# Routing steps placed by traced durations, expert weights split again at each visit, and tiles 2 to 7 turned through DRAM

## The chip, the cores and the metric

The kernel runs on one core of a Trainium2 chip. The metric is the device time of one execution in microseconds; lower is better. The engines are named as in the profile: PE (TensorE matmuls), PEld (its weight loads), DVE (VectorE), ACT (ScalarE), POOL (GpSimd) and SP (SyncE, which here only issues DMAs).

## The reference

A short causal filter, then a mixture of experts in which every token goes to exactly one of eight experts, by a greedy walk through all logits with a capacity for each expert.

```python
B, S, d_model = 8, 3584, 192                  # 28672 tokens; 8 heads of 24 columns, 7 taps
w = softmax(weight)                            # (8, 7)
x = einsum('hk,bskhg->bshg', w, windows(x))    # each head mixes 7 tokens

logits = x @ w_gate                            # (28672, 8)
order = np.argsort(-logits.flatten())
for idx in order:                              # greedy, capacity 3584 for each expert
    tok, e = idx // 8, idx % 8
    if assigned[tok] >= 0 or counts[e] >= cap: continue
    assigned[tok] = e; counts[e] += 1
for e in range(8):
    out[assigned == e] = np.maximum(x[assigned == e] @ w1[e], 0) @ w2[e]   # 192 -> 1024 -> 192
```

## The kernel before

**Two stages.** First the filter: 16 half-batches of 1792 tokens, each with 8 heads (PE matmul cv, ACT copy a, a DMA of the result to attn in DRAM), and the gate's logits beside it (pl, then LT). Then the feed-forward part: 56 tiles of 512 tokens, numbered from 0. Tiles 0 to 7 take one tile from each expert 0 to 7, tiles 8 to 31 three from each expert 7 down to 0, tiles 32 to 55 three from each expert 0 to 7. In run, each tile has eight steps: in step f, PE computes one eighth of the first layer of tile i (l1: five matmuls into ph, then ACT's relu hh and VectorE's remainder hl) and half of a quarter of the second layer of tile i-1 (l2: eight matmuls into y). All numbers are split into a high and a low part, so that float32r matmuls are accurate enough.

**Routing.** Which token goes where is found by generators (half(0), tail, half(1), rest) whose steps are put between the other work: thresholds, counts, a sort by one-hot matmuls (sort for the first half, sort4 for the others), a table read back from DRAM (otab, tile OT), a gather matmul (asm) and the decoding into token numbers (tokens, which writes ia, ja, ib, jb). The matmuls of these steps write the tile bg. sort4 makes one-hot tiles oa on VectorE, multiplies them on PE, ACT copies the result to X, and S.dma_start writes it to otab.

**What sets their place.** Instructions stand on each engine in the order in which the program emits them. Pace keeps an estimate of the time on PE, DVE and ACT, from the cost of each instruction in Meter. Steps.hook emits routing steps as long as VectorE's estimate is not more than slack ahead of PE's. A generator can yield PEW: its next step then comes only when PE's estimate has passed that of VectorE plus lat (0.8 in the feed-forward part). bg.drain emits all that is left at once: idx_of calls it in step 0 of tile 6 for half(1) and in step 0 of tile 30 for rest, since the gathers of tiles 8 and 32 need the lists.

**Tokens.** gather fetches a tile's tokens to xg two tiles ahead, with four indirect DMAs on POOL. They have to be turned for l1. Three ways: PE transposes into px (transp, evac: tiles 0 to 7), a turn through DRAM (turn, where swapped(i) is true: tiles 8 to 31; one VectorE transpose in step 6 of tile i-2, four writes to scr and two reads back on SP, then ACT copies in step 3 and subtracts in step 4 of tile i-1, the one for xa on POOL), and VectorE transposes alone (shuffle: tiles 32 to 55). The turn through DRAM needs the rows of the token list in another order, which tokens makes with sixteen small VectorE instructions (swap).

**Weights.** plan lists the pieces of each expert's weights, eight for a visit. wload brings a piece as it is to one of four raw tiles (SP), wsplit makes the high part on ACT and the low part on the engine eng (VectorE from tile 0 on). At an expert's first visit the split pieces are also written to DRAM (kw, kd, kv), and a later visit loads them split. Two sets of buffers alternate between visits.

Of the kernel before, what the change touches and what calls it, by code (L numbers as in the profile page):

```python
# [28 lines left out]
class Meter:  # L29
# [5 lines left out]
    def __getattr__(self, op):  # L35
# [4 lines left out]
        def call(*a, **k):  # L40
# [4 lines left out]
            if self.name == "pe":  # L45
                n = size(aps[2])

                d = n / 2400 * (0.25 if bf and size(aps[1]) == 32 else 1 if aps[2].dtype in (BF, FR) or size(aps[1]) == 32 else 2 if op == "transpose" else 4)
                p.pe += max(d + 0.0025, 0.027 if bf else 0.107)
# [195 lines left out]
TA = 16  # L245
# [13 lines left out]
class Route:  # L259
# [167 lines left out]
    def columns(self, h, nt, base):  # L427
# [9 lines left out]
        V.tensor_copy(bi[:, 1], ps[:, 0:8])  # L437
        V.tensor_scalar(bi, bi, 8, None, op0=OP.arith_shift_right)
# [34 lines left out]
    def sort(self, h, nt, base, per=8):  # L473
# [7 lines left out]
        while z < 128:  # L481

            t = max(q[0][1] + nc.las, free[0] if z % 32 == 0 else 0.0) if q else 0.0
            if q and t <= nc.pe:
                if z == 64:
                    self.columns(h, nt, base)
# [25 lines left out]
    def sort4(self, h, nt, base):  # L512
# [9 lines left out]
        free = [0.0, 0.0]  # L522
        while z < 8:

            t = max(q[1][1] + nc.las, free[0]) if len(q) > 1 else 0.0
            if len(q) > 1 and t <= nc.pe:
                if z == 4:
                    self.columns(h, nt, base)
                ps = self.bg()
                for v in range(2):  # L530
                    a = q.pop(0)[0]
                    for u in range(2):
                        for c in range(4):
                            j = 2 * v + u
                            PE.matmul(ps[32 * c:32 * c + 32, 128 * j:128 * j + 128],
                                      b[:, :, 32 * (c % 2) + 4 * z + j], a[:, u, :, c],
                                      start=True, stop=True, skip_group_check=True)
                A.activation(O[z // 4][:, 4 * (z % 4):4 * (z % 4) + 4].rearrange("p g q -> p (g q)"), ps, AF.Copy)
                free = [free[1], nc.act + nc.las]
                z += 1  # L540
                if z % 4 == 0:
                    S.dma_start(self.otab[z // 4 - 1], O[z // 4 - 1])
# [54 lines left out]
    def tokens(self, nt, idx, row, e1=8, t1=None, swap=False):  # L597
# [30 lines left out]
        if swap:  # L628
            r4, y4 = (t.rearrange("p e (t b) -> p e t b", b=4) for t in (row, y))
            for q in range(4):  # L630
                for b in range(4):
                    V.tensor_scalar(r4[32 * q:32 * q + 32, :, :, b], y4[32 * b:32 * b + 32, :, :, q], 4.0, None,
                                    op0=OP.mult)
                yield
        else:
            V.tensor_scalar(row, y, 4.0, None, op0=OP.mult)
            yield
# [15 lines left out]
    def counts(self, n0):  # L653
# [23 lines left out]
        yield  # L677
# [181 lines left out]
    def final(self):  # L859
# [32 lines left out]
        yield  # L892
# [254 lines left out]
class FFN:  # L1147
# [3 lines left out]
    def __init__(self, tc, nc, attn, w1, w2, out, ident, wr, drm):  # L1151
        self.tc, self.nc = tc, nc

        self.kept1 = [drm.tile([128, 3, F], F32, name="kw%d" % e) for e in range(NE)]
        self.keptd = [drm.tile([64, F], F32, name="kd%d" % e) for e in range(NE)]
        self.scr = [drm.tile([6, 32, 4, 128], F32, name="scr%d" % j) for j in range(2)]
        self.kept2 = [drm.tile([128, 8, 2 * D], F32, name="kv%d" % e) for e in range(NE)]
# [19 lines left out]
    def plan(self, tiles):  # L1177
# [7 lines left out]
        self.pieces = []  # L1185
        for j, ky in enumerate(keys):
            w = last[keys[j - 2]] + 1 if j > 1 else j - 1
            if ky[0] in [k[0] for k in keys[:j]]:
                self.pieces += [(w, ky, j % 2, "W1", 0), (w + 1, ky, j % 2, "W2", 0)]
                continue  # L1190
            for what, q in (("a", 0), ("d", 0), ("a", 1), ("d", 1)):
                self.pieces.append((w, ky, j % 2, what, q))
            for q in range(4):
                self.pieces.append((w + 1, ky, j % 2, "w", q))
        self.loaded = self.done = 0

    def wload(self):
        nc = self.nc
        if self.loaded == len(self.pieces) or self.pieces[self.loaded][3] in ("W1", "W2"):
            return  # L1200
        _, (e, _), _, what, q = self.pieces[self.loaded]
# [13 lines left out]
    def wsplit(self, i, eng):  # L1215

        if self.done == len(self.pieces) or self.pieces[self.done][0] > i:
            return
        V, A = self.nc.vector, self.nc.scalar
        _, ky, j, what, q = self.pieces[self.done]  # L1220
        wp = self.wpa[j]
        e = ky[0]
        if what == "W1" or (what, q) == ("a", 0):
            W = wp.tile([128, 3, F], FR, name="w1")
            self.WT[ky] = [W[:, 0], W[:, 1], W[:, 2], self.DL[j]]
        if what == "W1":
            self.nc.sync.dma_start(W.bitcast(F32), self.kept1[e])
            self.nc.sync.dma_start(self.DL[j][0:64].bitcast(F32), self.keptd[e])
            self.done += 1
            return  # L1230
        if what == "W2":
            t = self.wpb[j].tile([128, 8, 2 * D], FR, name="w2")
            self.WT[ky].append(t)
            self.nc.sync.dma_start(t.bitcast(F32), self.kept2[e])
            self.done += 1
            return
# [465 lines left out]
```

## Time and profile before

| | us |
|---|---|
| median of 3 runs | 1257.85 (1257.07 to 1260.27) |
| the profiled execution, its own time | 1263.32 |
| its span, first to last instruction | 1261.5 |
| PE busy | 1211.2 |
| DVE busy | 974.1 |
| ACT busy | 548.5 |
| POOL busy | 534.1 |

Busy time of PE is modelled from pipelined matmuls. L55 is the line of the helper that records each instruction, so almost all of VectorE's, ScalarE's and TensorE's work has that line, and the names of the tiles tell the operations apart (in the changed kernel the helper's line is L56). In a waits row the numbers are: us in total, how many times, the longest.

### The profile page before, as it was taken

Reading aid. Unit: us, or ns where it says so; the run is one execution under the profiler, and the core shown is the slowest. Engines: PE = TensorE matmul, PEld = TensorE weight load, DVE = VectorE, ACT = ScalarE, POOL = GpSimd, SP = SyncE. Lnnn points to the kernel's source line nnn. Section 1 sums busy time; section 2 is a strip of 40 time slices with the busy share of each in tenths; the row PEclk is TensorE's granted clock in tenths of the full one; section 3 lists DMA queues with packets and bytes.
Section 4 is the critical chain, followed back from the end, with each engine's and each line's share of the span. In section 5 each row is a group of like instructions: output and inputs, shape, how many; then the busy total and the mean of one; then the engine's idle time right before and its main releaser. Section 6 shows DMA issues by size and latency. Waiting matters only on the chain.

```text
span 1261.5 us, 21753 instructions
## 1 busy us (share of the span) xinstructions
PE 1211.2 (96%) x7702; PEld 1038.5 (82%) x7702; DVE 974.1 (77%) x2131; ACT 548.5 (43%) x1220; POOL 534.1 (42%) x528
## 2 busy tenths in 40 slices
PE   5989998999899999999899999999999999999997
PEld 2445567889799889888788999999999999999997
DVE  7398579899799999989885444777777777777772
ACT  4544655565345435454343333333333333333332
POOL 3000434354455454544534555444444444444422
PEclk9999999999899999999999999999999999999999
DMA  9999898899734443635274645113143232414100
GB/s 240 351 322 311 264 333 281 268 325 283 269 98 132 131 144 118 195 89 185 80 201 131 189 117 171 42 48 130 61 153 105 93 100 98 145 52 150 48 23 28
DMA packets 125188, 205.09 MB, mean 163 GB/s; under 512 B 21440, under 2 KB 85392, under 8 KB 121360
## 3 DMA queue, kind: packets, MB, share of 16 engines
q1 hardware_dynamic: 82464, 127.22, 31.6%
q0 software_dynamic: 21504, 44.07, 11.6%
q10 hardware_dynamic: 21104, 32.34, 7.8%
q8 instruction: 62, 1.02, 0.3%
q14 instruction: 54, 0.44, 0.1%
HBM read 118.64 MB, written 84.93 MB: 161 GB/s over the span
## 4 chain that ended last, share of the span: by engine, by line
PE 75%; DVE 13%; DMA 5%; issue 3%; SPq 1%; POOL 1%; ACT 1%; another core or an unknown queue 0%; DVEq 0%; POOLq 0%; ACTq 0%
PE ph L55 35%; PE y L55 34%; DVE X L55 4%; PE cv L55 3%; DVE hl L55 2%; PE bg L55 2%; DMA raw<-in_moe_w_dram 2%; DMA X<-in_x_dram 1%; DMA wgr<-in_moe_w_gate_dram 1%; DVE aT L55 1%; PE pl L55 1%; DVE oa L55 1%; DVE yo L55 1%; DMA kw<-w 0%; POOL xg L1269 0%
## 5 line engine op out<-in xcount | busy, mean ns | idle before, releaser
L55 PE MATMUL y<-w,hh 128*128 128x384 f32 x1792 | 537.7, 355 | 0.0
L55 ACT ACTIVATE hh<-ph 128x512 fp32r<-128x512 f32 x448 | 268.0, 598 | 478.3 <-PE ph L55 432.3
L55 PE MATMUL y<-w,hl 128*128 128x192 f32 x1792 | 449.6, 251 | 0.0
L55 DVE SCALAR_TENSOR_TENSOR hl<-ph,hh 128x512 fp32r<-128x512 f32 x448 | 307.6, 687 | 156.6 <-ACT hh L55 131.5
L55 PE MATMUL ph<-xa,w 128*128 128x512 f32 x1344 | 396.8, 403 | 0.7 <-DVE hl L55 0.6
L55 PEld LDWEIGHTS y<-w,hl 128*128 128x128 f32 x1792 | 341.9, 191 | 16.6
L55 PEld LDWEIGHTS y<-w,hh 128*128 128x128 f32 x1792 | 337.4, 188 | 22.0 <-issue 3.4
L1344 POOL DMA_INDIRECT out_dram<-yo,ia x128 | 142.5, 1113 | 258.7 <-DVE yo L55 222.4
L55 PEld LDWEIGHTS ph<-xa,w 128*128 128x128 f32 x1344 | 219.1, 189 | 21.8 <-issue 1.5
L1344 POOL DMA_INDIRECT out_dram<-yo,ib x96 | 96.0, 1000 | 220.0 <-DVE yo L55 212.6
L55 PE MATMUL ph<-xd,w 128*128 128x512 f32 x448 | 178.2, 398 | 1.1 <-DVE xd L55 1.1
L55 PE MATMUL ph<-xd,dl 128*128 128x512 f32 x448 | 174.9, 390 | 0.2 <-issue 0.2
L55 DVE STREAM_TRANSPOSE xs<-xg 32x128 f32<-32x128 f32 (+2 forms) x408 | 164.8, 404 | 6.6
L1269 POOL DMA_INDIRECT xg<-attn,ja x128 | 138.8, 1085 | 47.7 <-issue 39.0
L55 ACT ACTIVATE yt<-y 128x192 f32<-128x192 f32 x224 | 73.2, 327 | 103.5 <-PE y L55 84.8
L55 PE MATMUL cv<-X,TH 118*128 118x384 f32 x256 | 100.9, 520 | 16.9 <-DMA X<-in_x_dram 13.7
L1269 POOL DMA_INDIRECT xg<-attn,jb x96 | 103.5, 1078 | 29.3 <-issue 29.3
L55 DVE TENSOR_TENSOR yo<-y,yt 128x192 f32<-128x192 f32 x224 | 79.0, 353 | 41.7 <-ACT yt L55 37.6
L55 PEld LDWEIGHTS ph<-xd,w 128*128 128x128 f32 x448 | 84.4, 188 | 25.2 <-issue 4.7
L55 PEld LDWEIGHTS ph<-xd,dl 128*128 128x128 f32 x448 | 84.6, 189 | 20.2 <-issue 0.5
L55 PEld LDWEIGHTS cv<-X,TH 118*128 118x128 f32 x256 | 45.1, 197 | 50.4 <-issue 14.6
L55 ACT ACTIVATE a<-cv 128x384 f32<-128x384 f32 x128 | 59.8, 492 | 54.5 <-PE cv L55 41.8
(238 smaller groups left out, 886.1 us busy)
## 6 DMA issues: line engine op xcount, KB each, us to landing
attn<-a ACTq DMA_DIRECT2D x16, 1344.0 KB
w<-kw SPq DMA_DIRECT2D x14, 1536.0 KB
w<-kv SPq DMA_DIRECT2D x14, 1536.0 KB
kw<-w SPq DMA_DIRECT2D x48, 256.0 KB
kv<-w SPq DMA_DIRECT2D x32, 384.0 KB
X<-in_x_dram SPq DMA_DIRECT2D x17, 672.0 KB
X<-in_x_dram ACTq DMA_DIRECT2D x15, 672.0 KB
scr<-xs SPq DMA_DIRECT2D x96, 96.0 KB
```

Source lines behind the costliest of these rows:

```text
L55: return f(*a, **k)
L1269: self.nc.gpsimd.indirect_dma_start(out=t[:, b], out_offset=None, in_=self.attn[0:rows], in_offset=bass.IndirectOffsetOnAxis(ap=idx[b], ax ...
L1344: st = self.nc.gpsimd.indirect_dma_start(out=self.out, out_offset=bass.IndirectOffsetOnAxis(ap=idx, axis=0), in_=o, in_offset=None, bounds ...
```

## The change

It has four parts.

- Costs of the planner. VectorE: 0.15 + n/960 instead of the larger of 0.08 + n/960 and 0.18; ScalarE: 0.22 + n/1370 instead of 0.12 + n/1400; float32r matmuls 17/16 of before. Four waits PEW are added: in columns, after its first two instructions, in counts, in final, and so in sort and sort4, which call columns.
- sort4 emits its matmuls in four groups of 64, each when four one-hot tiles are there, instead of eight groups of 32 with two.
- Tiles 2 to 7 are turned through DRAM too. The first list (ja0) therefore gets the other row order, after a small list j2 for tiles 0 and 1 in the old order.
- kw, kd and kv are gone. Every visit loads raw pieces and splits them, later visits with the subtract on POOL, and with the next raw load issued two wsplit calls later (owed). A visit whose buffer still holds that expert (experts 6 and 1) loads nothing (same).

```diff
-                p.dve = max(p.dve, p.pe) + max(0.08 + n / 960 / w, 0.18)
+                p.dve = max(p.dve, p.pe) + 0.15 + n / 960 / w
             else:
-                p.act = max(p.act, p.pe) + 0.12 + n / 1400 + (0.2 if "accum_out" in k else 0)
+                p.act = max(p.act, p.pe) + 0.22 + n / 1370 + (0.2 if "accum_out" in k else 0)
...
         V.tensor_copy(bi[:, 1], ps[:, 0:8])
+        yield PEW
...
-            t = max(q[1][1] + nc.las, free[0]) if len(q) > 1 else 0.0
+            t = max(q[3][1] + nc.las, free) if len(q) > 3 else 0.0
...
+            if j > 1 and keys[j - 2][0] == ky[0]:
+                self.same[ky] = self.same.get(keys[j - 2], keys[j - 2])
+                continue
             w = last[keys[j - 2]] + 1 if j > 1 else j - 1
-            if ky[0] in [k[0] for k in keys[:j]]:
-                self.pieces += [(w, ky, j % 2, "W1", 0), (w + 1, ky, j % 2, "W2", 0)]
-                continue
+            again = ky[0] in [k[0] for k in keys[:j]]
...
+        self.turns += 1
+        while self.owed and self.owed[0] <= self.turns:
+            self.owed.pop(0)
+            self.wload()
...
+        if again:
+            eng = self.nc.gpsimd
...
         eng.tensor_tensor(lo, r[0:n], hi[0:n].bitcast(F32), op=OP.subtract)
-        S = self.nc.sync
-        if what == "w":
-            S.dma_start(self.kept2[e][:, s], t[4][:, s].bitcast(F32))
...
+        self.done += 1
+        if again:
+            self.owed.append(self.turns + 2)
         else:
-            S.dma_start(self.kept1[e][:, 2, s], hi.bitcast(F32))
-            S.dma_start(self.keptd[e][:, s], lo.bitcast(F32))
-        self.done += 1
-        self.wload()
+            self.wload()
...
     def swapped(self, i):
-        return self.tiles[i][1][1] in (1, 2, 3)
+        return i > 1 and self.tiles[i][1][1] < 4
...
         def first():
             for e in range(2):
-                ff.gather(e, [ja0[:, e, b:b + 1] for b in range(4)], NTOK // 2, P)
+                ff.gather(e, [j2[:, e, b:b + 1] for b in range(4)], NTOK // 2, P)
+            drain(r.swapped(ja0, r.y))
```

Where the steps stand then. In the filter, four of the five count matmuls of the threshold move one to three heads later. half(1) has its sort in tiles 3 and 4 instead of tile 2, its gather in tile 4 instead of tile 3. The first round has its matmuls in tile 9 instead of 7, the last two sorts stand in tiles 27 to 29 instead of 22 to 24.

On PE, at the end of routing, before: the end of the step that precedes the last gather (bg from iq and then from c_oh), in tile 24. The last sort matmuls stand five steps earlier.

```order
L55 MATMUL ph<-xa,w_7098 128x512 x3
L55 MATMUL ph<-xd,w_7098 128x512
L55 MATMUL ph<-xd,dl 128x512
L55 MATMUL y<-w_7355,hh 128x384
L55 MATMUL y<-w_7355,hl 128x192
...
L55 LDWEIGHTS ones
L55 MATMUL bg<-iq,ones 128x192
L55 LDWEIGHTS X_8487
L55 MATMUL bg<-c_oh,X_8487 128x24
```

And in the changed kernel, at the end of tile 29: the first row is the last matmul of the last sort; between it and the gather stand eight y matmuls, of which two are shown.

```order
L56 MATMUL bg<-oa,X_9192 32x128
L56 MATMUL y<-w_7892,hh 128x384
L56 MATMUL y<-w_7892,hl 128x192
...
L56 LDWEIGHTS ones
L56 MATMUL bg<-iq,ones 128x192
L56 LDWEIGHTS X_9655
L56 MATMUL bg<-c_oh,X_9655 128x24
```

The distance from the last sort to the gather has shrunk from five steps to half a step.

On SP, in one of the first tiles, before: raw loads, each behind the writes of the piece split before.

```order
L1255 DMA kw_87<-w_2991 128x512
L1256 DMA kw_87<-w_2991 128x512
L1210 DMA raw<-in_moe_w_dram 128x2x192
L1258 DMA kw_87<-w_2991 128x512
L1259 DMA kd_95<-dl 64x512
L1210 DMA raw<-in_moe_w_dram 128x2x192
```

And in the changed kernel, around step 6 of one of the first tiles:

```order
L1222 DMA raw<-in_moe_w_dram 128x2x192 x2
L1392 DMA scr_83<-xs 32x6x128 x4
L1394 DMA xs<-scr_83 128x512
L1395 DMA xs<-scr_83 64x512
L1222 DMA raw<-in_moe_w_dram 128x2x192 x2
L1217 DMA raw<-in_moe_w_dram 128x512
```

The writes to kw, kd and kv are gone, and one raw load a tile now stands behind the six transfers of the turn.

On POOL, before, around tile 11: the gather of four indirect DMAs (xg), the scatters of results (out_dram) and the subtract for xa.

```order
L1269 DMA xg<-attn,ja 128x192 x4
L1344 DMA out_dram<-yo,ia 28672x192 x2
L1403 TENSOR_TENSOR xa<-xs,xa 128x512
L1344 DMA out_dram<-yo,ia 28672x192 x2
L1269 DMA xg<-attn,ja 128x192 x4
```

And in the changed kernel, tile 11:

```order
L1269 DMA xg<-attn,ja 128x192 x4
L1256 TENSOR_TENSOR w_4696<-raw,w_4696 128x512
L1344 DMA out_dram<-yo,ia 28672x192
L1256 TENSOR_TENSOR dl<-raw,w_4696 64x512
L1256 TENSOR_TENSOR w_4696<-raw,w_4696 128x512
L1344 DMA out_dram<-yo,ia 28672x192
L1256 TENSOR_TENSOR dl<-raw,w_4696 64x512
L1403 TENSOR_TENSOR xa<-xs,xa 128x512
L1344 DMA out_dram<-yo,ia 28672x192 x2
```

Four subtracts for the weights have come in between the gather and the subtract for xa.

More of the change, by code (lines that the diff above doesn't have):

```diff
@@ L485, in sort @@
                 if z == 64:
-                    self.columns(h, nt, base)
+                    yield from self.columns(h, nt, base)
                 a = q.pop(0)[0]
@@ L1318, in l2 @@
         hh, hl = self.H[i]
[L1319 removed]
+        w = self.wt(key)[4]
         if half == 0:
```

106 lines of the change are left out of this document (49 added, 57 removed).

## The prediction

> **What bounds the kernel now.** I read the page first, for the share of each engine and the chain that ended last.
>
> ```profile
> span 1261.5 us, 21753 instructions
> PE 1211.2 (96%) x7702; PEld 1038.5 (82%) x7702; DVE 974.1 (77%) x2131; ACT 548.5 (43%) x1220; POOL 534.1 (42%) x528
> PE 75%; DVE 13%; DMA 5%; issue 3%; SPq 1%; POOL 1%; ACT 1%; another core or an unknown queue 0%; DVEq 0%; POOLq 0%; ACTq 0%
> ```
>
> TensorE is busy for 96% of the span and is three quarters of the chain, so time changes only where PE works longer, waits, or runs at a lower clock. To see where, I cut the feed-forward part into windows whose edges are the starts of a tile's first ph matmul in the timeline. A tile has 104 matmuls of its own (40 into ph, 64 into y). The columns are the window, its length, then busy time and count for PE, PEld, DVE, ACT, POOL, and the granted clock, the DMA share and GB/s.
>
> ```profile
> 175.88:199.96 24.08, 22.16 (x146) 19.07 (x146) 19.17 (x46) 11.76 (x25) 3.65 (x5) 1.00 0.89 314
> 199.96:227.58 27.62, 25.45 (x244) 21.17 (x243) 26.66 (x52) 15.37 (x30) 15.12 (x9) 1.00 0.85 275
> 269.17:288.36 19.19, 19.19 (x114) 17.36 (x113) 18.95 (x40) 14.24 (x38) 11.04 (x10) 1.00 0.95 325
> 288.36:307.57 19.21, 19.21 (x114) 17.37 (x113) 18.73 (x47) 10.60 (x22) 7.20 (x8) 1.00 0.96 310
> 307.57:332.71 25.14, 21.95 (x112) 19.52 (x111) 20.39 (x49) 10.29 (x23) 12.50 (x12) 0.86 0.84 272
> 332.71:600.98 268.27, 265.65 (x1538) 238.35 (x1536) 249.19 (x573) 126.61 (x322) 138.86 (x126) 1.00 0.45 140
> 600.98:629.65 28.67, 25.37 (x218) 21.60 (x216) 24.28 (x57) 9.81 (x20) 14.04 (x14) 0.94 0.28 79
> 629.65:654.17 24.52, 24.30 (x239) 20.96 (x236) 21.37 (x40) 11.13 (x22) 7.95 (x7) 1.00 0.67 186
> 654.17:677.45 23.28, 21.84 (x190) 19.14 (x188) 14.94 (x36) 8.97 (x18) 10.36 (x10) 1.00 0.71 207
> 677.45:1244.54 567.09, 567.09 (x3226) 514.73 (x3225) 395.92 (x825) 217.09 (x433) 253.21 (x244) 1.00 0.30 99
> ```
>
> The last row is tiles 25 to 55: 567.09/31 = 18.29 us a tile with PE never idle. That is the floor, and no edit lowers it. The rows above are tile 1, 2, 5, 6, 7, then 8 to 21 together, then 22, 23, 24. All that can be won or lost lies in what they have above 18.29. Next, whom PE waited for:
>
> ```profile
> PE bg L55 <- DVE r_cc L55: 5.5, 4, 3.2
> PE bg L55 <- DVE m_x L55: 4.1, 5, 1.0
> PE bg L55 <- DVE c_bi L55: 2.3, 2, 2.0
> PE px L55 <- DVE xa L55: 2.1, 2, 1.4
> PE bg L55 <- issue: 2.1, 2, 1.2
> PE bg L55 <- DVE u_b L55: 2.1, 1, 2.1
> PE bg L55 <- DVE k_c L55: 1.2, 1, 1.2
> ```
>
> All are routing matmuls (bg) or transposes of gathered tokens (px) for which VectorE was late: DVE is busy 249.19 of 268.27 us in tiles 8 to 21, more than the planner's costs allow for.
>
> **The change, part by part.**
>
> (a) PE transposes. Tiles 2 to 7 go through DRAM, so tiles 1 to 6 lose eight transposes each. Tiles 5 and 6 hold these and no routing matmul, and take 19.19 and 19.21: 0.90 us above 18.29. Six times that: -5.4. In their place stands, on VectorE, one transpose:
>
> ```profile
> L55 DVE STREAM_TRANSPOSE xs<-xg 128x768 f32<-128x768 f32 x24 | 23.2, 966 | 0.0
> ```
>
> It comes (0.97) instead of one of two subtracts; the other subtract stays, and the first goes to POOL. ACT's two copies stay. SP gets four writes and two reads a tile, see (c).
>
> (b) The two px waits on DVE belong to those transposes and go with them: -2.1.
>
> (c) Tile 7. This is the timeline there, and then the two windows of low clock, with the columns of the windows above:
>
> ```profile
> 315.80 0.29 SPq L1210 DMA_DIRECT2D raw<-in_moe_w_dram  x1
> ...
> 319.59 0.53 ACT L55 ACTIVATE w<-raw 128x384 fp32r<-128x384 f32 x1 [4.59 <-DMA raw<-in_moe_w_dram]
> ...
> 321.24 1.93 DVE L55 TENSOR_TENSOR X<-X 128x448 bf16<-128x448 bf16 x3
> 321.26 1.49 POOL L1403 TENSOR_TENSOR xa<-xs,xa 128x512 fp32r<-128x512 f32 x1 [4.80 <-ACT xa L55]
> ...
> 323.52 0.21 PE L55 MATMUL bg<-r_cc,ones 128*128 128x56 bf16 x1 [3.19 <-DVE r_cc L55]
> ...
> 328.83 0.99 DVE L55 TENSOR_TENSOR X<-X 128x448 bf16<-128x448 bf16 x3
> ```
>
> ```profile
> 322.98:329.81 6.83, 6.29 (x20) 5.61 (x20) 6.32 (x17) 1.67 (x4) 1.67 (x2) 0.50 0.76 271
> 606.25:609.70 3.45, 3.45 (x12) 2.69 (x12) 2.57 (x6) 0.16 (x1) 0.14 (x1) 0.51 0.26 98
> ```
>
> A raw weight load issued at 315.80, behind scr transfers and kw writes on SP's queue, came late. ACT stood for 4.59, DVE behind it, and PE waited 3.19 and then worked 6.3 us at half clock (loss 3.2). With 0.2 of routing left in the tile, 25.14 - 18.29 - 0.2 = 6.6. The kw, kd and kv writes vanish, and in the new order PE has no routing matmul between tiles 4 and 9: -6.6. What is late next is the same load in tiles 0 to 6, since each now has scr transfers ahead of one raw load; that load is needed four steps (9.1 us) later, and without routing matmuls behind it a short ACT wait costs PE nothing. In tiles 1, 3 and 4 it could; that is in (d)'s upper end.
>
> (d) The wait on c_bi (2.0 of it in tile 2) and on k_c gets a planner's wait of its own, and the DVE costs are now near the traced ones. 2.3 + 1.2 = 3.5 at best; if VectorE is as late as before, none; with raw loads late in three tiles, 1.5 lost. I take -2.5, nearer the rows.
>
> (e) The waits on m_x in the convolution (4.1 in five): four of the five matmuls move 1 to 3 heads later. -2, between 0 and -4.1.
>
> (f) Tiles 8 to 28, weights. Twelve visits cost ACT 8 copies and POOL 8 subtracts each, in place of two large loads; two visits drop out, because the buffer still holds that expert.
>
> ```profile
> L1403 POOL TENSOR_TENSOR xa<-xs,xa 128x512 fp32r<-128x512 f32 x24 | 32.1, 1336 | 38.2 <-ACT xa L55 36.9 <-PE bg L55 1.0 <-issue 0.2
> L1269 POOL DMA_INDIRECT xg<-attn,ja x128 | 138.8, 1085 | 47.7 <-issue 39.0 <-PE px L55 7.3 <-PE ph L55 0.8
> L55 ACT ACTIVATE w<-raw 128x512 fp32r<-128x512 f32 x32 | 20.1, 628 | 9.4 <-DMA raw<-in_moe_w_dram 8.3 <-issue 1.0
> ```
>
> ACT gains 4 x 0.63 = 2.5 us in a loaded tile on 126.61/14 = 9.0: covered. POOL has 138.86/14 = 9.9 a tile, about 0.3 of issue before each of 8 indirect DMAs, and now 4 x 1.34: 9.9 + 2.4 + 5.4 = 17.7 of 18.29. It keeps up, and every third tile has none. If that cover goes, gathers come late and VectorE's transposes wait. SP issues a raw load two steps after the split and stands if POOL has not yet read the buffer: POOL's fourth subtract ends some 4 x 1.38 + 5.4 + 2 x 1.4 = 13.7 us into the tile, as step 6 puts the scr transfers behind that load (6/8 x 18.29 = 13.7). That is covered, with nothing to spare. What is not covered is VectorE itself: beside the POOL subtract at 321.26 three DVE instructions took 1.93, and without one 0.99. So a hit costs 0.94. Six of the visits, 48 subtracts, fall into tiles 11 to 28 while routing runs, 8 in every three tiles; with the planner's margin of 0.8 most should not reach PE. The waits on r_cc besides tile 7 are 5.5 - 3.19 = 2.3. I take them as twice that: +2; ends -2.3 and +8 (one hit in six getting through whole, 48/6 x 0.94 = 7.5).
> The Trainium skill ("SBUF — State Buffer", section "SBUF: two separate sides") says that VectorE with two SBUF inputs and GpSimd take one port pair in turn, each for a whole instruction. The trace agrees with 1.93 against 0.99; priced at a whole subtract of 1.34 instead of 0.94, (f) would be +2.9 and the sum 0.9 higher.
>
> (g) Tiles 22 to 24, now 27 to 29: u_b 2.1, half clock after it 3.45/2 = 1.7, and the two "issue" waits inside the sort 2.1, which now starts only when four one-hot tiles are there. 5.9 at best, 2 if half stays with no clock loss; I take -4.5.
>
> (h) The last gather. Routing now runs to the end of tile 29, where the planner must finish it. In the new order only the eight y matmuls of half a step (18.29/16 = 1.1 us) stand on PE between the last sort matmul and the gather matmul that reads the table back from DRAM. Before, five steps stood there:
>
> ```profile
> 632.13 1.19 PE L55 MATMUL bg<-oa,X 128*32 128x128 bf16 x32
> 635.58 3.76 SPq L559 DMA_DIRECT2D X<-otab  x8
> 644.07 0.26 PE L55 MATMUL bg<-iq,ones 128*128 128x192 bf16 x1
> 660.69 1.19 PE L55 MATMUL bg<-oa,X 128*32 128x128 bf16 x32
> 661.43 1.09 ACT L55 ACTIVATE X<-bg 128x512 bf16<-128x512 f32 x2 [0.58 <-PE bg L55]
> 662.54 0.32 SPq L542 DMA_DIRECT2D otab<-X  x1
> 662.97 8.34 SPq L559 DMA_DIRECT2D X<-otab  x8
> 674.13 0.55 PE L55 MATMUL bg<-c_oh,X 128*128 128x24 bf16 x16 [0.56 <-DMA X<-otab]
> ```
>
> The last sort matmul ended at 660.69 + 1.19 = 661.88, and PE got the table at 674.13: 12.25 us, less 1.1 is 11.1. In the sort before, the last read was issued by 639.34, 6.0 after the sort's end at 633.32, so at least 4.9. I take 9.5, near the later row, since scr transfers stand ahead on SP there too. After it comes half clock, 1.7 to 3.2: +12, between +6.6 and +14.3. VectorE's decoding of the list then stands before the next hl, which PE needs only a tile later.
>
> Sum: -5.4 - 2.1 - 6.6 - 2.5 - 2 + 2 - 4.5 + 12 = -9.1 us. The profiled execution took 1263.32 us, so 1254.2 there; it is 5.5 above the median of 1257.85, and on the median it is 1248.7. About 0.3% (3.8 us) is what a measurement of this kernel can tell from no change.
>
> **Rivals.** Slower: POOL's subtracts stop VectorE in tiles 11 to 28 and PE feels it. If half the 48 get through at 0.94, that is 22.6 in place of the +2 of (f): 1269. It decides from about 16 of 48 on ((12.9 + 2)/0.94, to 0.3% slower). For it speaks the 1.93; against it that 24 such subtracts stand in the trace of before, with r_cc waits of 5.5 in all.
>
> The planner's new costs don't do what they should: VectorE stays late by other causes (ACT behind raw loads, POOL), so (d), (e) and (g) give nothing, +9.0: 1257.7, no change.
>
> The last gather is mostly hidden: with SP free, no 1.5 MB load on the queue and 4.9 of waiting, (h) is 6.6 or, if the table lands within the next steps, about 4: 1240.7.
>
> **How the numbers follow.** The sum as worked out has 0.50, the hidden gather 0.14, the planner without effect 0.17, POOL's collisions 0.11; 0.08 is left for the unlisted, split evenly. Faster is 0.50 + 0.14 and most of the rest with part of the planner's case: 0.72; same 0.15; slower 0.13. The ends of (d) to (h) reach from about -21 to +1 around the sum without all falling one way: 1238 to 1260; the forecast's own range is 1242 to 1255.
>
> **What would show it.** Tiles 5 and 6 at 18.3 (a); no px wait on DVE and no half clock near tile 7 (b, c); waits on c_bi, k_c and u_b near zero (d, g); r_cc waits of some 4 us, with long DVE rows beside POOL's L1256 (f); one PE wait of about 10 us on X<-otab just before tile 30, with half clock behind it (h). The forecast is wrong if that wait is absent or PE waits in tiles 11 to 28 add up to more than 10 us.

## The result, and the profile after

| | us |
|---|---|
| before, median of 4 runs on the same chip | 1258.23 (1257.07 to 1260.27) |
| after, median of 4 runs | 1275.88 (1274.33 to 1279.28) |
| ratio | 1.0142, 95% interval 1.0118 to 1.0167 |
| after, the profiled execution and its span | 1275.91 and 1274.0 |

The change makes the kernel 1.4% slower; 1248.7 was forecast. From the page of the changed kernel, the lines that answer to the first three of before (span; busy time, share and count of each engine; the chain that ended last by engine):

```profile
span 1274.0 us, 22016 instructions
PE 1209.8 (95%) x7654; PEld 1035.6 (81%) x7654; DVE 1015.5 (80%) x2147; ACT 589.6 (46%) x1316; POOL 652.8 (51%) x630
PE 71%; DVE 16%; DMA 6%; issue 4%; ACT 2%; SPq 1%; POOL 1%; DVEq 0%; ACTq 0%; POOLq 0%
```

PE is busy 1.4 us less, VectorE's busy time is 41.4 us more although it has only 16 instructions more, and VectorE's share of the chain has grown from 13% to 16%. The same windows by tile, with the columns as before; rows are tiles 1, 2, 5, 6, 7, then 8 to 21, 22 to 26, 27 to 29, and 30 and 31:

```profile
180.21:202.25 22.04, 20.97 (x138) 18.21 (x138) 17.92 (x42) 11.86 (x26) 8.71 (x8) 1.00 0.67 186
202.25:220.65 18.40, 18.40 (x108) 16.69 (x106) 17.16 (x34) 9.67 (x20) 8.16 (x8) 1.00 0.57 164
263.20:282.89 19.69, 18.54 (x107) 16.62 (x105) 17.90 (x46) 10.41 (x22) 7.34 (x8) 1.00 0.57 161
282.89:301.18 18.29, 18.29 (x107) 16.61 (x105) 16.52 (x38) 10.30 (x22) 9.77 (x10) 1.00 0.66 187
301.18:319.99 18.81, 18.61 (x107) 16.55 (x105) 15.97 (x29) 10.64 (x29) 10.04 (x9) 1.00 0.63 181
319.99:594.41 274.42, 265.59 (x1508) 237.92 (x1507) 250.97 (x545) 133.36 (x319) 178.42 (x159) 0.99 0.38 108
594.41:697.96 103.55, 96.77 (x556) 86.33 (x555) 93.78 (x167) 51.40 (x128) 66.24 (x59) 0.98 0.37 103
697.96:778.37 80.41, 69.66 (x639) 60.11 (x638) 61.86 (x121) 32.17 (x64) 34.51 (x31) 0.95 0.42 122
778.37:816.41 38.04, 38.04 (x214) 34.39 (x212) 24.37 (x59) 13.71 (x27) 18.83 (x19) 0.96 0.14 42
```

From tile 32 on each takes 18.29 us as before. The table has what each stage takes above 18.293 us a tile (the start and the convolution in full), worked out from such windows; "waits" are PE's idle times over 0.15 us in it:

| stage | before | after |
|---|---|---|
| start and convolution | 158.8 | 164.2 |
| tiles 1 to 7 | 28.8 | 11.7 |
| routing's rounds | 12.2 (tiles 8 to 21; waits 2.5) | 30.4 (tiles 8 to 26; waits 15.6) |
| last sorts and gather | 21.6 (tiles 22 to 24; waits 5.0) | 27.0 (tiles 27 to 31; waits 10.8) |

Tiles 1 to 7 gain the 17 us that were forecast. The rounds lose 18.2, the stretch up to tile 0 5.5 (4.3 of it in the convolution), the end of routing 5.4. A selection from the waits of PE names all three (X for the end, r_cc, F and hl for the rounds, aT and m_x for the convolution):

```profile
PE bg L56 <- DMA X<-otab: 10.6, 1, 10.6
PE bg L56 <- DVE r_cc L56: 8.3, 7, 3.0
PE bg L56 <- DVE F L56: 5.1, 3, 3.9
PE pl L56 <- DVE aT L56: 4.1, 6, 2.2
PE ph L56 <- DVE hl L56: 2.7, 4, 1.2
PE bg L56 <- DVE m_x L56: 1.3, 3, 0.8
```

**The rounds.** This is the timeline in tile 17, ahead of the longest r_cc wait but one: start, length, engine, instruction, and in brackets the idle time before it.

```profile
497.44 1.30 POOL L1256 TENSOR_TENSOR dl<-raw,w 64x512 fp32r<-64x512 f32 x1
497.58 1.25 DVE L56 TENSOR_SCALAR r_x<-r_x 128x8 f32<-128x8 f32 x2
...
499.20 0.17 DVE L56 TENSOR_SCALAR r_dd<-r_d 128x8 f32<-128x8 f32 x1
499.41 0.28 DVE L56 TENSOR_TENSOR X<-j,r_dd 128x120 f32<-128x120 f32 x1
499.47 1.37 POOL L1256 TENSOR_TENSOR w<-raw,w 128x512 fp32r<-128x512 f32 x1 [0.73 <-ACT w L56]
499.61 1.27 DVE L56 TENSOR_SCALAR r_dd<-r_d 128x8 f32<-128x8 f32 x1
...
502.80 1.51 POOL L1256 TENSOR_TENSOR dl<-raw,w 64x512 fp32r<-64x512 f32 x1 [0.72 <-ACT w L56]
503.21 2.72 DVE L56 TENSOR_TENSOR X<-X 128x480 bf16<-128x480 bf16 x2
504.28 1.42 POOL L1403 TENSOR_TENSOR xa<-xs,xa 128x512 fp32r<-128x512 f32 x1
505.97 0.37 DVE L56 TENSOR_TENSOR r_cc<-X 128x120 bf16<-128x120 bf16 x1
506.39 0.21 PE L56 MATMUL bg<-r_cc,ones 128*128 128x120 bf16 x1 [2.68 <-DVE r_cc L56]
```

r_dd takes 0.17 when it starts with POOL at rest, and 1.27 when it starts 0.14 after a subtract of POOL: it ends (500.88) when the subtract does (500.84). The two r_x, 1.25 in all, the same. I call such an instruction held. X<-X, 2.72 for two, stands beside a third subtract and then beside the one for xa, which was in the kernel before too. PE stands 2.68 for the r_cc at the end of this chain.

**The end of routing**, at the end of tile 29:

```profile
769.01 0.34 SPq L1394 DMA_DIRECT2D xs<-scr  x1
769.39 0.45 SPq L1395 DMA_DIRECT2D xs<-scr  x1
769.89 0.58 SPq L546 DMA_DIRECT2D otab<-X  x1
770.57 5.37 SPq L563 DMA_DIRECT2D X<-otab  x8
777.95 0.58 PE L56 MATMUL bg<-c_oh,X 128*128 128x24 bf16 x16 [10.55 <-DMA X<-otab]
```

PE stands 10.55 us for the table. The granted clock is half from 771.1 to 781.4, but PE works only from 777.95 on, so this costs 1.7: 0.2 in tile 29, and in tiles 30 and 31 the 1.45 that they take above their floor (last row of the windows above: 38.04 us, PE never idle, clock 0.96).

**The convolution.** Its last blocks wait for VectorE's transposes aT, which stand behind held instructions and the sixteen of the swap (ja):

```profile
141.72 1.29 POOL L1256 TENSOR_TENSOR w<-raw,w 128x512 fp32r<-128x512 f32 x1 [32.52 <-ACT w L56]
141.78 1.26 DVE L56 TENSOR_SCALAR m_i<-m_f,off 128x32 int32<-128x32 f32 x1
...
145.41 3.12 DVE L56 TENSOR_SCALAR ja<-m_y 32x8 int32<-32x8 f32 x16
148.54 3.56 DVE L56 STREAM_TRANSPOSE aT<-a 128x768 f32<-128x768 f32 x4
149.66 0.40 PE L56 MATMUL pl<-aT,c_mu 128*32 128x128 f32 x2 [2.16 <-DVE aT L56]
```

Behind the wait the clock is half from 149.9 to 156.7, which costs 3.0. Over the whole convolution PE is idle 12.4 us before and 12.3 after, since the waits on m_x have shrunk; work at half clock costs 1.7 before and 6.0 after. So the 4.3 are half clock: these 3.0, and 1.3 more at 30 to 37 us, near the start.

### The profile page after: what moved, and what is told of

It is laid out like the page before. It is cut to its first block, busy times and chain, and to the rows that moved or that the text cites. A ratio compares the mean times of both kernels' runs of the same rounds, so it can differ in the third digit from the quotient of the medians.

```text
span 1274.0 us, 22016 instructions
## 1 busy us (share of the span) xinstructions
PE 1209.8 (95%) x7654; PEld 1035.6 (81%) x7654; DVE 1015.5 (80%) x2147; ACT 589.6 (46%) x1316; POOL 652.8 (51%) x630
## 4 chain that ended last, share of the span: by engine, by line
PE 71%; DVE 16%; DMA 6%; issue 4%; ACT 2%; SPq 1%; POOL 1%; DVEq 0%; ACTq 0%; POOLq 0%
PE ph L56 33%; PE y L56 31%; DVE X L56 5%; PE cv L56 3%; DVE hl L56 3%; PE bg L56 3%; DMA X<-in_x_dram 2%; DMA raw<-in_moe_w_dram 2%; DVE aT L56 1%; PE pl L56 1%; DMA wgr<-in_moe_w_gate_dram 1%; DVE yo L56 1%; DVE xs L56 1%; DVE w L56 0%; DVE xd L56 0%
## 5 line engine op out<-in xcount | busy, mean ns | idle before, releaser
L56 DVE STREAM_TRANSPOSE xs<-xg 32x256 f32<-32x256 f32 (+2 forms) x414 | 170.6, 412 | 6.6
L1269 POOL DMA_INDIRECT xg<-attn,ja x120 | 127.2, 1060 | 46.0 <-issue 35.2
L56 PE MATMUL cv<-X,TH 118*128 118x384 f32 x256 | 103.5, 530 | 18.9 <-POOL TH L152 12.6
L1256 POOL TENSOR_TENSOR w<-raw,w 128x384 fp32r<-128x384 f32 (+1 forms) x74 | 82.8, 1122 | 48.4 <-ACT w L56 47.3
L56 ACT ACTIVATE w<-raw 128x512 fp32r<-128x512 f32 (+1 forms) x160 | 91.4, 571 | 28.1 <-DMA raw<-in_moe_w_dram 28.1
```

The costliest lines, as they stand in the source:

```text
L56: return f(*a, **k)
L1256: eng.tensor_tensor(lo, r[0:n], hi[0:n].bitcast(F32), op=OP.subtract)
L1269: self.nc.gpsimd.indirect_dma_start(out=t[:, b], out_offset=None, in_=self.attn[0:rows], in_offset=bass.IndirectOffsetOnAxis(ap=idx[b], ax ...
```

## The experiments

Chips differ, so the ratio to the kernel before on the same chip stands with each result. The kernel before took 1258.79 us (median) beside the first four experiments, 1270.10 beside the next four, 1268.24 beside the third four and 1270.44 beside the last three.

**1. No subtract at later visits.** ScalarE writes the low part as a second copy; the order on the other engines is unchanged.

```diff
-        eng.tensor_tensor(lo, r[0:n], hi[0:n].bitcast(F32), op=OP.subtract)
+        if again:
+            self.nc.nc.scalar.activation(lo, r[0:n], AF.Copy)
+        else:
+            eng.tensor_tensor(lo, r[0:n], hi[0:n].bitcast(F32), op=OP.subtract)
```

> The changed kernel, but at later visits the low part of the weights is made by a ScalarE copy of the raw piece instead of POOL's subtract (so the low part is not the residual; the computation is changed in that). The order on PE and VectorE is the same as in the changed kernel. Theory port (POOL's subtracts hold up VectorE's routing instructions in tiles 8 to 28, and PE waits for those): PE's waits on VectorE in tiles 8 to 26, 15.6 us in the changed kernel, fall to 4 or less, the half clock there goes, and the time falls by 12 to 17, to 1259 to 1264. Theory plan (the new costs, waits and the loaded ScalarE make routing late, whoever subtracts): ScalarE has 96 copies more, so 1273 or more, waits unchanged.

Measured: 1254.52 us, ratio 0.9965 (0.9948 to 0.9982). That is 21.4 below the kernel after, more than the 12 to 17 of the theory. PE's waits on r_cc fall from 8.3 to 1.5, those on F from 5.1 to 0.3. Tiles 8 to 26 as one window, of this kernel:

```profile
317.80:677.40 359.60, 357.96 (x2063) 321.42 (x2061) 311.79 (x711) 202.70 (x491) 192.59 (x173) 1.00 0.40 112
```

and of the kernel after:

```profile
319.99:697.96 377.97, 362.36 (x2062) 324.25 (x2061) 344.75 (x711) 184.76 (x447) 244.66 (x217) 0.99 0.38 107
```

The same 711 VectorE instructions take 33.0 us less without POOL's 44 subtracts in that window (20 of 128x384, 12 of 128x512, 12 of 64x512; 1.18 us each in the mean): 0.75 for each subtract. The window is 18.4 us shorter: 0.42 of each reached the end. A loaded ScalarE was not what held, since it is 18 us busier here. This run takes load off POOL too, so by itself it doesn't exclude that late gathers held; experiment 10 does.

**2. The old weights**, with all else as after: kw, kd and kv written at the first visit and loaded at the later ones.

```diff
+            if ky[0] in [k[0] for k in keys[:j]]:
+                self.pieces += [(w, ky, j % 2, "W1", 0), (w + 1, ky, j % 2, "W2", 0)]
                 continue
...
-            again = ky[0] in [k[0] for k in keys[:j]]
...
+        if what == "w":
+            S.dma_start(self.kept2[e][:, s], t[4][:, s].bitcast(F32))
...
```

> The changed kernel with the weights as before: written split to DRAM at the first visit, loaded split later. Theory port: the waits of tiles 8 to 26 fall to 4 or less, and the last gather has three steps ahead of it (wait of about 5 instead of 10.5); a wait near tile 7 may come back (up to 6): 1256 to 1264. Theory plan: waits in tiles 8 to 26 stay at 12 or more: 1268 to 1276.

Measured: 1269.24, ratio 1.0080 (1.0056 to 1.0104). Tiles 8 to 26 have 13.0 above the floor and waits of 1.3, as the theory of the port says. But tiles 1 to 7 have 38.7 in place of 11.7, with waits of 18.5: ACT's w waits for raw are 67.8 us in all (28.1 in the kernel after), and raw loads now stand behind kw and kv writes and the scr transfers of six more tiles. By that the time lies above the 1256 to 1264 of the theory.

**3. The old costs** of the planner, with all else as after.

```diff
...
-                p.dve = max(p.dve, p.pe) + 0.15 + n / 960 / w
+                p.dve = max(p.dve, p.pe) + max(0.08 + n / 960 / w, 0.18)
...
-                p.act = max(p.act, p.pe) + 0.22 + n / 1370 + (0.2 if "accum_out" in k else 0)
+                p.act = max(p.act, p.pe) + 0.12 + n / 1400 + (0.2 if "accum_out" in k else 0)
```

> The changed kernel with the planner's old costs in Meter (the added waits and the new grouping of the sort stay). Routing then ends in tile 26 and the last gather stands five steps behind its sort. Theory port: the wait of 10.5 at tile 30 goes with its half clock (-12), but VectorE is later against the plan and still held up by POOL, so the waits in tiles 8 to 23 are 15 or more: 1264 to 1272. Theory plan: the new costs were what made the kernel slower: 1258 or less.

Measured: 1286.31, ratio 1.0211 (1.0181 to 1.0242): 10.4 above the kernel after, where both theories said below it. Routing ends in tile 26 and the table's wait is 2.2, but the rounds and sorts have 63.4 above the floor with waits of 26, and tiles 1 to 7 have 19.4. The dearer costs are worth these 10.4 us in this kernel. That they do it by leaving a reserve, which takes up part of what POOL does to VectorE, is my reading.

**4. The gather of tile 32 later** (step 5 of tile 30 instead of step 0), so that routing's end is drained later.

```diff
-                if i + 2 < n and f == 0:
+                if i + 2 < n and f == (5 if i == 30 else 0):
```

> The changed kernel, but the gather of tile 32 is issued in step 5 of tile 30 instead of step 0, so that routing need not be finished at once; the last gather matmul then stands in step 4 of tile 30. If the wait of 10.5 is the price of the deadline alone: it and its half clock go, -10 to -12, 1264 to 1266. Rival, that the time comes back because VectorE turns tile 32 later: 1270 or more, with a wait in tile 31 or 32.

Measured: 1266.20, ratio 1.0063 (1.0038 to 1.0087): 9.7 below the kernel after. The table's wait is 2.1 instead of 10.6.

**5. The kernel before, profiled once more.**

> The kernel before, profiled once more, to see which of its stages made the profiled execution of the prediction 4.5 us longer than the median. If the stall of tile 7 (a raw load that came late) was an accident of that one execution, tiles 5 to 7 have 2 to 3 us above their floor of 18.29 each instead of 8.7, and term (c) was mostly not there to win. If it is the kernel's own, they have 8 to 9 again and the difference lies in the rounds of tiles 8 to 24.

Measured: 1269.90 in one run, on a chip where its median is 1270.10. Tiles 5 to 7 have 9.2 above the floor; ACT waits 5.78 for the raw load and PE 3.94 behind it. The stall of tile 7 is in both traces, so it is the kernel's own, and (c) was there to win.

**6. The old turn** of tiles 2 to 7, without the swap; all else as after.

```diff
-        return i > 1 and self.tiles[i][1][1] < 4
+        return self.tiles[i][1][1] in (1, 2, 3)
...
-            drain(r.swapped(ja0, r.y))
```

> The kernel after, but tiles 2 to 7 turned by TensorE as before, and without the 16 small instructions that reorder the first list at the end of the convolution. Routing is then emitted to the end of tile 29 with five steps between the last sort matmul and the matmul that reads its table. Theory (turning through DRAM is worth 0.9 us a tile, the reordering costs 3.1 us of VectorE in front of the convolution's last blocks, the last gather was exposed): against the kernel after +5.4 and up to +2 in tiles 1 to 7, -3 in the convolution (148 to 149 instead of 151.7), -10 to -12 at tile 29: 1265 to 1270 us. Rival (the transfers through DRAM cost SP's queue as much as they save TensorE): tiles 1 to 7 no longer than in the kernel after, 1260 to 1263 us.

Measured: 1274.01, ratio 1.0024 (1.0002 to 1.0046), against 1.0142 for the kernel after. The convolution takes 147.2 (151.7 after), the table's wait is 2.75. Tiles 1 to 7 have 14.7 above the floor, 15.6 in the kernel after on a like chip (experiment 9), so the transposes come back without a loss there: PE is busy 142.30 instead of 140.32, of which 1.7 is half clock, so 3.7 us of transposes, and its waits are 0.5 instead of 2.9. Term (a) is a real saving of PE's work, but on these chips the waits and the half clock of the turn through DRAM (2.4 and 1.7) take all of it back. The rival of the expectation was right on that. (In the first trace of the kernel after, tiles 1 to 7 have no half clock and 11.7.)

**7. The swap behind the convolution**; all else as after.

```diff
-            drain(r.swapped(ja0, r.y))
...
         for f in left + todo:
             f()
+        drain(r.swapped(ja0, r.y))
```

> The kernel after, with the 16 small instructions that reorder the first list emitted behind the convolution instead of in front of its last blocks; the rest of routing is then planned a few steps later. One look for the convolution's length. Theory (its 4.3 us are 3.1 of these instructions on VectorE and about 2 of VectorE instructions held beside GpSimd's subtracts): 148.3 to 149.3 us between the first convolution matmul and the first matmul of tile 0, where the kernel after takes 151.7. Rival (GpSimd's subtracts alone, or scalar copies in front of the convolution's evictions): 151 to 152 as it is.

Measured: the convolution takes 146.6 us, below the theory's 148.3 and far from the rival's 151. One and the same convolution differs by some 3 us between traces, but over all of them it takes 146.6 to 150.6 without the swap in front of its last blocks (six traces: the kernel before, its second profile, experiments 6, 7, 8 and 13) and 150.7 to 154.3 with the swap there on VectorE (ten). The held instructions in front of it are in experiments 6 and 7 too (m_i takes 1.26 in both), and there the convolution is no longer than before. So it is the swap that lengthens it, by some 4 us: 3.1 of VectorE more in front of aT, and then the half clock behind PE's wait. (The 1283.63 us of this one run come from a routing that ends still later, with 34.6 above the floor in tiles 27 to 29.)

**8. A first version** meant to be better: the low part of later visits on VectorE up to tile 30, the gather of tile 32 at step 6, the swap behind the convolution, and more slack.

```diff
-        if again:
+        if again and i > 30:
             eng = self.nc.gpsimd
...
-        SS = (1.8, 3)
+        SS = (4.5, 5)
```

> The kernel after with four edits drawn from the runs so far: the low part of an expert's later visits is subtracted on VectorE (in the planner's sight) while routing still runs and on GpSimd from tile 31 on; the rows of tile 32 are gathered at step 6 of tile 30; the 16 reordering instructions stand behind the convolution; the planner's slack is 4.5 and 5 in place of 1.8 and 3, so that the last sort ends four steps ahead of its gather. Theory: convolution -3, rounds of tiles 8 to 26 excess 30 to 12 or 16, the last gather -10: 1243 to 1250 us. Rival (VectorE, 93% busy there, pays for the eight subtracts what GpSimd's collisions cost): 1256 to 1262 us.

Measured: 1271.58, ratio 1.0009 (0.9990 to 1.0027): not the gain expected. The convolution takes 150.0. Tiles 8 to 26 are as the theory has them (16.3), but tiles 1 to 7 have 27.2 and tiles 27 to 31 have 25.9: the slack holds for the first lists too, and VectorE runs so late that ph waits 9.6 us on hl.

**9. The kernel after, once more**, on another chip.

> The kernel after itself, once more beside the kernel before, since chips differ (the kernel before took 1258 us on one and 1270 on another). Expected: 16 to 20 us longer than before on the same chip (ratio 1.012 to 1.017), as first measured; stages as in the first trace. If the ratio comes out under 1.005, what was measured first belongs to the chip and not to the change.

Measured: 1286.23, ratio 1.0150 (1.0108 to 1.0192). The loss belongs to the change and not to the chip. Tiles 1 to 7 have 15.6 above the floor, tiles 8 to 26 34.9, tiles 27 to 31 30.5.

**10. A one-input instruction on POOL** in place of the subtract.

```diff
+        if again:
+            eng.tensor_scalar(lo, r[0:n], 1.0, None, op0=OP.mult)
+        else:
+            eng.tensor_tensor(lo, r[0:n], hi[0:n].bitcast(F32), op=OP.subtract)
```

> The kernel after, but at an expert's later visits GpSimd writes the low part as a plain product of the raw weights by 1 (one SBUF input) instead of the residual (two inputs); the order of all instructions is unchanged, and the low part is not the residual. Theory (GpSimd's two-input instructions stop VectorE while they run): with one input they don't, tiles 8 to 26 fall from 30 us above their floor to 12 to 14, and the time is 17 to 21 us under the kernel after. Rival A (any GpSimd instruction of that length stops VectorE): within 5 us of the kernel after. Rival B (GpSimd's load makes gathers late, whatever the instruction): also within 5 us, with the waits on xa, xd or xs instead of r_cc.

Measured: 1279.19, ratio 1.0088 (1.0054 to 1.0122), 7.0 below the kernel after on the same chip. That lies between the theory and its rivals; tiles 8 to 26 have 24.1 above the floor, 34.9 in experiment 9. Rival B is not what is seen: PE waits 9.9 us on r_cc and 1.3 on xd, as in experiment 9 (10.7 and 1.3), though POOL is as busy. The rows say that rival A is right in part (timeline of this kernel in tile 17):

```profile
506.78 1.52 POOL L1257 TENSOR_SCALAR dl<-raw 64x512 fp32r<-64x512 f32 x1
506.87 0.72 DVE L56 TENSOR_SCALAR r_d<-r_tl,Ts 128x8 f32<-128x8 f32 x1
507.62 0.71 DVE L56 TENSOR_SCALAR r_dd<-r_d 128x8 f32<-128x8 f32 x1
508.25 1.50 POOL L1257 TENSOR_SCALAR w<-raw 128x512 fp32r<-128x512 f32 x1
508.37 0.65 DVE L56 TENSOR_TENSOR X<-j,r_dd 128x120 f32<-128x120 f32 x1
508.94 0.16 DVE L56 TENSOR_SCALAR r_dd<-r_d 128x8 f32<-128x8 f32 x1
```

The second r_dd, in the middle of POOL's instruction, takes 0.16, so a one-input instruction does not keep VectorE off to its end; but r_d and the first r_dd take 0.72 and 0.71. VectorE is busy 327.80 in tiles 8 to 26, where the kernel after has 341.68 on that chip: about half of the stretching goes. How a one-input instruction holds VectorE for a part of its length stays open.

**11 and 12. Two versions** with the slack raised for routing's last part alone (2.5 and 3), the low part on VectorE up to tile 30, tile 32's gather at step 6; in the second the swap on ScalarE.

```diff
-        if again:
+        if again and i > 30:
...
-                bg.hook(SS[0], 4, SS[1])
+                z = SS if len(bg.gens) > 1 else (2.5, 3)
+                bg.hook(z[0], 4, z[1])
```

> The kernel after with the low part of later visits on VectorE (metered by the planner) up to tile 30 and on GpSimd behind it, tile 32's rows gathered at step 6 of tile 30, and the slack of routing's last part 2.5 instead of 1.8, so that its last sort ends four to five steps ahead of its gather; nothing else changed in the convolution and tiles 0 to 7. Theory: excess of tiles 8 to 26 from 30 to 12 to 17 us, the last gather's wait from 10.5 to 0 to 4: 18 to 26 us under the kernel after, ratio to before 0.994 to 1.000. Rival (VectorE is full there, so its own eight subtracts in every three tiles cost as much): within 6 us of the kernel after.

Measured: 1268.68, ratio 1.0010 (0.9989 to 1.0031), 17.6 below the kernel after there. Tiles 8 to 26 have 13.6, as the theory has it, so eight subtracts on VectorE in every three tiles cost little. But routing ends in a drained sort at step 5 of tile 30, and the table's wait is still 7.4.

> The same as v2_mix, with the 16 small instructions that reorder the first list on ScalarE instead of VectorE. Theory (they hold up the last transposes of the convolution by 3.1 us on VectorE): the convolution 2 to 3 us shorter, and so the time. Rival (on ScalarE they hold up the convolution's evictions as long): no difference to v2_mix within 1 us.

Measured: 1268.41, ratio 1.0014 (0.9992 to 1.0036). The convolution takes 154.9 (153.9 in v2_mix): on ScalarE the swap is no better, as the rival says, with the 8.2 us that PE waits there on ACT's a (3.2 in v2_mix).

**13. The subtracts alone, added to the kernel before**: 44 of them on POOL in tiles 9 to 24, all of 128x512 (1.32 us each) and on two spare buffers that POOL fills once; no load, copy or DMA is added, and no other engine's order is changed.

```diff
+                    if 8 <= i <= 24 and i % 3 < 2 and f < 4:
...
+                    G.tensor_tensor(self.junk[1], self.junk[0], self.junk[1], op=OP.subtract)
```

> The kernel before, with 44 subtracts of 128x512 that nothing needs added on GpSimd in tiles 9 to 24 (four steps in each of two tiles out of three, about where the changed kernel has its own), between two spare buffers; the order on all other engines is unchanged, no raw load, scalar copy or DMA is added. Theory (such subtracts stop VectorE for 0.8 to 0.9 us each, 36 us of stretched VectorE rows in tiles 8 to 26 of the kernel after, and half of it reaches TensorE): 44 x 0.85 = 37 us more VectorE time and 15 to 20 us more in all, ratio 1.012 to 1.016. Rival (the loss of the kernel after comes from raw loads, the scalar copies or the chain of an expert's pieces between them, and the subtract alone is covered): within 5 us of the kernel before.

Measured: 1310.48, ratio 1.0296 (1.0254 to 1.0337): 40 us, twice the theory's 15 to 20. Tiles 8 to 26 of this kernel,

```profile
338.10:762.40 424.30, 387.15 (x2383) 341.90 (x2381) 372.44 (x740) 170.96 (x409) 246.68 (x217) 0.97 0.43 127
```

and of experiment 5, on another chip with the same median of before:

```profile
333.80:721.00 387.20, 373.73 (x2383) 333.32 (x2381) 329.75 (x740) 169.86 (x409) 188.27 (x171) 1.00 0.45 139
```

VectorE's 740 instructions take 42.7 us more, 0.97 a subtract, and the window is 37.1 longer: 0.84 a subtract. The subtracts alone make such a loss, with no weights behind them. With the old costs of the planner 87% of the held time reaches the end; with the new ones 56% (18.4 of 33.0). The subtracts differ in length and place too, so no run shows how much of that the costs do.

**14 and 15. The end of routing by slack alone**, after v2_mix: with the low part on VectorE up to tile 25 and slack 3 and 4, and with slack 6.

```diff
-        if again:
+        if again and i > 25:
...
+                z = SS if len(bg.gens) > 1 else (3, 4)
```

> v2_mix with the low part of later visits on VectorE up to tile 25 only and the slack of routing's last part 3 and 4: the last sort is then emitted to the second step of tile 30 and its gather's matmul three steps later. Theory: tiles 8 to 26 as in v2_mix (13 to 15 us above their floor), the wait on the table 7.4 and the drained sort in tile 30 gone, a few held VectorE rows in tiles 26 to 30: 8 to 14 us under v2_mix, ratio to before 0.990 to 0.995. Rival (the larger slack lets VectorE run so late that the feed-forward's own matmuls wait on hl): 0 to 5 us under v2_mix, with hl waits of several us in tiles 8 to 30.

Measured: 1263.30, ratio 0.9945 (0.9920 to 0.9970): faster than the kernel before by 0.55%, and than the kernel after (ratios 1.0142 and 1.0150) by some 2%. Its sort's end and gather, in tile 30:

```profile
766.69 1.18 PE L56 MATMUL bg<-oa,X 128*32 128x128 bf16 x32
777.61 0.26 PE L56 MATMUL bg<-iq,ones 128*128 128x192 bf16 x1
777.70 0.55 PE L56 MATMUL bg<-c_oh,X 128*128 128x24 bf16 x16
```

From the last sort matmul's end, 767.87, to the gather's start are 9.8 us of other work, and PE doesn't wait for the table.

> v2_mix with the slack of routing's last part 6 in place of 2.5 and 3, the low part on VectorE up to tile 30: the last sort is emitted to the second step of tile 30 too. Theory: as v4, 8 to 14 us under v2_mix, without the held rows in tiles 26 to 30. Rival (slack 6 lets VectorE run up to 6 us late, which the one buffer between ScalarE and VectorE doesn't cover): hl waits of 5 to 15 us in tiles 8 to 30, and no gain on v2_mix.

Measured: 1268.63, ratio 0.9978 (0.9961 to 0.9994). The gather is hidden here too, but the rounds have 19.1 above the floor (14.5 in v4), and tiles 5 to 7 have 7.4 (2.1 in v4). PE waits 11.4 us on hl (6.2 in v4). So the rival holds in part: more slack than needed is paid for.

## Why the prediction was wrong

**(f), POOL's subtracts: +2 forecast, +16.5 measured** (tiles 8 to 26: waits 15.6 and half clock 3.4, less the 2.5 of before; experiment 1 has 18.4). This is the step that failed. The price of a hit, 0.94, was of the right size: in the mean over all subtracts 0.75 in the kernel after, 0.97 in experiment 13. The failed sentence is "with the planner's margin of 0.8 most should not reach PE". I reckoned with 2 us out of 48 x 0.94. A mean so near the price says that most subtracts hit, and 56% of the held time came out at the end. VectorE is busy over 90% of tiles 8 to 21 (249.19 of 268.27 us before), so it has little room for 0.9 us more; that this fullness is the reason is my reading, no run varies it by itself. The rival "half the 48 get through", priced at 22.6 us for (f) and given a chance of 0.11, is what happened in kind: 18.4 of 33.0. The evidence against it was that 24 such subtracts stood in the trace of before; but 5.5 us of r_cc waits stood there too, and they said what one in a while costs, not what four in a row do. I had also counted two-input instructions alone. The Trainium skill ("SBUF — State Buffer", section "Who interferes with whom") says that tensor_scalar can take the shared port pair too, in its two-port modes; r_dd's 1.27 against 0.17 beside a subtract agrees. It also says that the loser is blocked for the whole instruction; the subtracts here agree, the one-input products of experiment 10 do not (r_d ends in the middle of one).

**(e), the convolution: -2 forecast, +4.3 measured** (151.7 in place of 147.3). The waits on m_x did fall, from 4.1 to 1.3, but without the swap the convolution takes 147.2 and 146.6 (experiments 6 and 7), so that was worth 0.7 at most, not 2. What the sum left out is the swap: sixteen instructions drained at one place in front of aT. The code shows them, and I gave them no row; nor did I show PE's wait on aT, which the trace of before has once, with 1.4 us, and the trace after six times, with 4.1.

**(h), the last gather: +12 forecast, 12.3 measured** (wait 10.6, half clock 1.7): right in place, kind and size. Experiment 4 took 9.7 of it away by one number.

**(a) to (d): -16.6 forecast, -17.05 measured in tiles 1 to 7.** (b), (c) and (d) happened: no px wait, no half clock near tile 7, c_bi and k_c gone. Experiment 5 shows that the stall is in the kernel, experiment 2 that it takes the absence of the kw and kv writes, and experiment 3 that without the new costs 7.7 of the 17 are lost. (a) is right for PE's work by itself (3.7 instead of 5.4), but experiment 6 has tiles 1 to 7 as short without it. So that the sum agrees to half a microsecond is luck in part; between experiments 5 and 9, on other chips, it is -14.2.

**(g), the sorts: -4.5 forecast, -6.5 measured**: waits of 5.0 and 1.7 of half clock before; besides the gather's, 0.2 after.

**The step from profile to median.** The sum was made against a profiled execution that ran 5.5 us over its median, and I took the 5.5 off. The spans differ by 12.5, the medians by 17.65: the profiled run of after stands at its own median. So 5.1 of the miss of 27.2 us come from the sample; where they lay in the run of before, no run here shows. Of the rest, 14.5 lie in (f) and 6.3 in (e), the other terms give back 2.2, and 3.5 belong to no term.

The forecast's own test, "PE waits in tiles 11 to 28 add up to more than 10 us", was met: they are 15.3.

## What to carry to other kernels

Before giving GpSimd work that reads SBUF, look at what VectorE does in that stage, not only at how free GpSimd is. Where VectorE was 85% to 93% busy, with routing among it, each subtract on GpSimd (1.0 to 1.5 us long) cost 0.75 to 0.97 us of VectorE, and 56% to 87% of it came out at the end. From tile 32 on the same subtracts cost nothing. These are two tiles' worth of time of the kernel after, the first without a subtract on GpSimd and the second with four:

```profile
853.00:871.29 18.29, 18.29 (x106) 16.61 (x105) 14.03 (x31) 7.02 (x14) 8.35 (x9) 1.00 0.14 44
871.29:889.58 18.29, 18.29 (x106) 16.61 (x105) 14.04 (x31) 9.11 (x18) 13.49 (x13) 1.00 0.30 87
```

VectorE is 77% busy there, and its 31 instructions take as long beside the subtracts as without them: none is held. So fullness is not the whole of it; which instructions VectorE runs counts too. What runs beside the four subtracts here are the remainders hl, transposes and the outputs yo; the two that subtract one SBUF tile from another (xa, xd) come 5 us behind the last of the four subtracts.

The same subtracts on VectorE itself, where the planner sees them, were cheaper (13.6 above the floor in tiles 8 to 26 of v2_mix, 34.9 in experiment 9 on the same chip). And when a plan makes work later, look for the next deadline that it runs into: one number at the last gather was worth 9.7 us, while the dearer costs that moved the sorts there were worth 10.4 by themselves.

## What was not expected of the hardware

VectorE instructions of 128x8 elements with one input, 0.16 to 0.17 us by themselves, take up to 1.27 beside a two-input subtract on GpSimd, and 0.71 beside a one-input product of 1.5 us. The same program differs by 1% between chips: the kernel before took 1258 to 1259 us in the first measurement and beside experiments 1 to 4, and 1268 to 1270 on three other chips, with instructions of equal length and longer waits in between (PE is busy 1211.2 us in both profiles, VectorE 974.1 and 974.8).
